# One norm-row buffer spaced over eight score steps, and a second store buffer and a fourth raw buffer for the weights

## The chip, the cores and the metric

The kernel runs on one core of one Trainium2 chip. The metric is the device time of one execution in microseconds; lower is better. Before the change three runs took 1256.49, 1258.76 and 1260.37 us, median 1258.76 us.

## The reference

The program is an attention block, followed by two chained dense blocks, all in float32:

```
attn_setup: batch, n_heads, seq, head_dim = (4, 12, 448, 64)
q_n, k_n = rmsnorm(q, g_q), rmsnorm(k, g_k)        # x / sqrt(mean(x*x) + 1e-6) * g
attn = softmax(1/sqrt(64) * q_n @ k_n^T)
x = (attn @ v), heads joined to (1792, 768)
h = ((x @ w1) * (x @ w2)) @ w3 ; x = h @ w_out      # first block, d_ff 1024
h = x @ w_in ; g = h * clip(h + 3, 0, 6) / 6        # second block, d_ff 2048
out = g @ w_out2
```

The kernel replaces `w3 @ w_out` by one product W' (768 x 1024), which it computes itself while attention runs.

## The kernel before

Attention works on 24 head pairs. A pair takes eight score steps of 112 query rows each, so there are 192 steps; pair i owns steps 8i to 8i+7. A step is: two score matmuls (lines 549 and 550), one VectorE pass that scales the scores by the norms' rows `rb` and takes the row maximum (556), a ScalarE exponential (568), and eight steps later the transposes (575), their split into a high and a low part (584, 594) and the product with V (627, 628).

TensorE gets two kinds of work: these steps, and "filler", cut into groups of three matmuls (lines 81 to 83, the `mm3` helper, which splits a float32 product into three passes). Filler is first W' (`wprime`, 128 groups), then for each batch `layer1` (96 groups, reads `xhl`) and `layer2` (48 groups, reads `abh`). `fill` hands filler out after each step, by a rate in microseconds. Filler needs weights that are converted on the chip: a raw piece (`raw`) comes in by DMA, ScalarE (137, 138) and VectorE (140, 143) turn it into float32, ScalarE takes the high part (203 for W', 287 for layer 1) and GpSimd the low part (205, 289); then the raw buffer is free and the next piece is fetched. Layer 1's converted weights go back to DRAM (`w12d`) and are read again for later batches. W' leaves PSUM in `evac`: ScalarE (223) and VectorE (224) write the store buffer `wst`, and three DMAs store it to `wpd`.

The norms: `load_nat(i)` brings the 112x1024 rows of q and k of pair i, `ssq` squares them in place on ScalarE (446), `ssum` sums them on VectorE (453). For every second pair `rms1`, `rms2`, `small1` and `small2` turn the sums of two pairs into the factors, store them to `rkd`, and `load_rb` reads them back as the rows `rb` that line 556 needs.

Which task is traced at which step stands in the list at the end of `attention` (`at(t, ...)`), moved by the table `SHIFT` (`ssum` one step earlier, `rms1` one later, among others). A scheduler then sets the final order on each engine from its own model of the time: what it holds to be ready first goes first. Filler may not come before the matmuls of three steps earlier (`issue_after`), but it may come much later than where it was traced. Each engine works through its list in order, and SyncE (SP) issues all DMAs, also in order, so an instruction that waits holds all that stand behind it.

After attention the second block runs: conversion and split of its weights with 512 + 512 groups of matmuls, from about 656 us on.

Of the kernel before, what the change touches and what calls it, by code (L numbers as in the profile page):

```python
# [26 lines left out]
P = 128  # L27
CP = 112
# [19 lines left out]
def fused_kernel(ctx: ExitStack, tc: tile.TileContext, nat, qT, kT, vin, gq, gk,  # L48
# [48 lines left out]
    def at(t, fn, *a):  # L97
        tasks[max(t + SHIFT.get(getattr(fn, "__name__", ""), 0), now[0])].append((fn, a))
# [117 lines left out]
    def wprime():  # L216
        pool, place = W["pool"], W["place"]

        def evac(a, n, ps):
            h = NH // P  # L220
            st = pool.tile([P, h, 2, P], F32R, tag="wst", bufs=1, name="wst")
            src = ps[:, :NH].rearrange("p (n c) -> p n c", c=P)
            nc.scalar.activation(st[:, :, 0, :], src, AF.Copy)
            nc.vector.tensor_sub(st[:, :, 1, :], src, st[:, :, 0, :])
            for i in range(h):
                j, c = divmod((n * h + i) * M1 + a, 6)
                dma(wpd[j, :, c], st[:, i].bitcast(F32).rearrange("p t c -> p (t c)"))

        def mul(a, n, c, ps):
            h, l = W["w3"][a, c // 4]  # L230
            cs = slice(c % 4 * P, c % 4 * P + P)
            wh, wl = W["woh"][c, n]
            mm3(ps[:, :NH], h[:, cs], l[:, cs], wh, wl, c == 0, c == M1 - 1)

        def ready(a, n, c):
            return prep[0].ready(place["a", a, c // 4]) and prep[0].ready(place["c", c, n])

        for group in [(0, 1)] + [(a,) for a in range(2, M1)]:
            for n in range(2):
                acc = [bank("f") for _ in group]  # L240
                for c in range(M1):
                    for a, ps in zip(group, acc):
                        while not ready(a, n, c):
                            yield None
                        mul(a, n, c, ps)
                        yield 3 * 0.163
                    if n == 1 and c % 4 == 3:
                        W["free"] += len(group)
                for a, ps in zip(group, acc):
                    later(evac, a, n, ps)  # L250
        yield None
        yield None
        W["cm"].__exit__(None, None, None)
        open_l1()
# [5 lines left out]
    def open_l1():  # L260
        L["cm"] = tc.tile_pool(name="l1", bufs=1, side="right", **RW)
        pool = L["cm"].__enter__()
        raw, ws = defaultdict(list), {}
        L.update(ws=ws, xhl={}, abh={}, cur=0, pool=pool)
        pieces = [(u, h) for u in range(2, 2 * M1) for h in range(2)]
        pieces.reverse()

        def load():
            if pieces:
                u, h = pieces.pop()  # L270
                raw[u].append(fetch(pool, w12[u // 2, 1 - u % 2][:, h * NH : h * NH + NH], NH, "raw", 3))

        def item(u):

            if u < 2:
                ws[u] = W["first"][1 - u]
                return
            r = u % NU
            t = (W["hp"] if u % 5 < 2 else pool).tile([P, 2, DM], F32R, tag="ws", bufs=2 if u % 5 < 2 else 3, name="ws")
            if u < 2 * M1:  # L280
                for h, f in enumerate(raw.pop(u)):
                    cs = slice(h * NH, h * NH + NH)
                    if f.dtype != F32:
                        w = f[:, :, 0]
                        yield from convert(w, f)
                        f = w.bitcast(F32)
                    nc.scalar.activation(t[:, 0, cs], f, AF.Copy)  # L287
                    yield 0.35
                    nc.gpsimd.tensor_sub(t[:, 1, cs], f, t[:, 0, cs])  # L289
                    load()  # L290
                    yield 0.0
                dma(w12d[r // 2, 1 - r % 2], t.bitcast(F32).rearrange("p t c -> p (t c)"))
            else:
                src = w12d[r // 2, 1 - r % 2] if r < 2 * M1 else wpd[r - 2 * M1].rearrange("p k c -> p (k c)")
                dma(t.bitcast(F32).rearrange("p t c -> p (t c)"), src)
                yield 0.0
            ws[u] = t

        for _ in range(3):
            load()  # L300
        prep[0] = Prep([partial(item, u) for u in range(B * NU)], lambda: L["cur"] + AHEAD)
        for _ in range(4):
            prep[0].step()
# [103 lines left out]
    def attention(ap, rate):  # L407
# [2 lines left out]

        def load_nat(i):
            if i < NP:
                T["nat", i] = ap.tile([CP, 4 * NC, D], F32, tag="nat", bufs=2, name="nat")
                a = T.get(("kl", i - 2))
                with ExitStack() as es:
                    if a is not None:
                        es.enter_context(tc.issue_after(a.ins))
                    dma(T["nat", i], nat[i].rearrange("p a b d -> p (a b) d"))
# [241 lines left out]
        groups = {s: [s, s + 1] for s in range(0, NP, 2)}  # L660

        load_nat(0)
        load_nat(1)
        dma(gs[:, 0:1], gq)
        dma(gs[:, 1:2], gk)
        nc.vector.tensor_mul(G, gs[:, 0:1], gs[:, 1:2])
# [25 lines left out]
        for z in range(16):  # L692
            prep[0].step()
        load_nat(2)
        load_nat(3)

        for i in range(NP):
            t = 8 * i
            n = i + 1
            if n < NP:  # L700
                at(t, qhi, n)
                at(t + 1, qlo, n)
                at(t + 2, ksplit, n)
            at(t - 4, load_v, i)
            if i + 2 < NP:
                at(t + 3, load_q, i + 2)
                at(t + 5, load_k, i + 2)
            at(t + 1, vsplit, i)
            if i % 2 == 0 and i + 2 < NP:
                g = groups[i + 2]  # L710
                at(t, ssq, i + 2)
                at(t + 2, ssq, i + 3)
                at(t + 3, ssum, i + 2, g)
                at(t + 3, load_nat, i + 4)
                at(t + 4, ssum, i + 3, g)
                at(t + 4, load_nat, i + 5)
                at(t + 5, rms1, g)
                at(t + 6, rms2, g)
                at(t + 14, load_rb, i + 3)

            u = t + LG
            at(u + 2, rsum1, i)
            at(u + 6, xcopy, i, 0)
            at(u + 7, xadd, i, 0)
            at(u + 8, small1, i, None)
            at(u + 9, small2, i, None)
            at(u + 9, xcopy, i, 1)
            at(u + 10, xadd, i, 1)
            at(u + 14, xout, i)
            if i % 2 == 0 and i + 2 < NP:  # L730
                g = groups[i + 2]
                tasks[t + LG] = [z for z in tasks[t + LG] if z[0] is not small1]
                tasks[t + LG + 1] = [z for z in tasks[t + LG + 1] if z[0] is not small2]
                at(t + LG, small1, i - 1, g)
                at(t + LG + 1, small2, i - 1, g)
# [212 lines left out]
```

## Time and profile before

| | |
|---|---|
| median of three runs | 1258.76 us |
| the profiled execution, its own time | 1259.43 us |
| its span, first to last instruction | 1257.6 us |
| TensorE busy | 1169.0 us (93%) |
| VectorE, ScalarE, GpSimd busy | 753.4, 727.0, 465.0 us |
| mean granted TensorE clock | 0.98 of full speed |
| DMA moved | 203.72 MB |

TensorE is busy nearly all the time in the later two thirds of the span; before about 390 us it is not, and there VectorE and ScalarE are busy for 80 to 90% of the time. So the table's averages hide two parts with different limits, and the rows below are cut by stretches.

### The profile page before, as it was taken

The page shows a single profiled execution, that of the slowest core. Times are in us where ns is not written, and L with a number is a line of the kernel's source. Part 1 is how long each engine was busy: PE and PEld are TensorE (multiplying, and loading weights), DVE is VectorE, ACT ScalarE, POOL GpSimd, SP SyncE. Part 2 cuts the span into 40 slices and gives each one's busy share as a digit, 9 for nine tenths or more (in the row PEclk, how much of TensorE's full clock was granted, in tenths as well). Part 3 has the DMA queues.
Part 4 walks back from the last instruction along what each step waited for, and adds up shares of the span by engine and source line. Part 5 has one row for each costly group of instructions (what it writes and reads, how often), then busy time and mean ns, then how long its engine had stood idle before and what let it go on. Part 6 is the DMA issues. An engine that isn't in the chain of part 4 may idle for free.

```text
span 1257.6 us, 16852 instructions
## 1 busy us (share of the span) xinstructions
PE 1169.0 (93%) x5868; PEld 1024.5 (81%) x5868; DVE 753.4 (60%) x1428; ACT 727.0 (58%) x1401; POOL 465.0 (37%) x292
## 2 busy tenths in 40 slices
PE   3688987887989999999999999899999999999998
PEld 2457976766678999899998998788999999999997
DVE  7887987899884487687623445775433343343332
ACT  6887886888774477677533435664534353444342
POOL 3444343554352022231020003445544554455542
PEclk9798998999999999999999999999999999999999
DMA  8777656598789577666359883440200020001001
GB/s 263 251 224 229 187 176 207 159 280 262 240 274 312 192 242 238 234 218 201 133 197 416 317 302 118 154 156 26 88 1 1 1 88 1 1 1 45 1 1 45
DMA packets 64693, 203.72 MB, mean 162 GB/s; under 512 B 8544, under 2 KB 25440, under 8 KB 64608
## 3 DMA queue, kind: packets, MB, share of 16 engines
q1 hardware_dynamic: 64608, 202.65, 48.4%
q8 instruction: 46, 0.75, 0.2%
q14 instruction: 39, 0.32, 0.1%
HBM read 173.93 MB, written 28.68 MB: 161 GB/s over the span
## 4 chain that ended last, share of the span: by engine, by line
PE 57%; DMA 5%; DVE 3%; ACT 3%; issue 3%; POOL 0%; SPq 0%; ACTq 0%; POOLq 0%; DVEq 0%
PE bank L81 6%; PE bank L82 6%; PE bank L83 6%; PE acc L82 6%; PE acc L81 6%; PE acc L83 6%; PE h L81 5%; PE h L82 5%; PE h L83 5%; DMA wr<-in_win_dram 2%; PE bank L575 2%; DVE wf L143 1%; DMA wr<-in_wo_dram 1%; PE bank L550 1%; PE bank L549 1%
## 5 line engine op out<-in xcount | busy, mean ns | idle before, releaser
L816 POOL TENSOR_TENSOR wis<-wf,wis 128x768 fp32r<-128x768 f32 x63 | 121.2, 1923 | 235.7 <-ACT wis L815 235.7
L888 DVE SCALAR_TENSOR_TENSOR u<-u,h 128x448 f32<-128x448 f32 x64 | 39.6, 618 | 212.1 <-ACT u L887 212.1
L556 DVE CUSTOM_DVE_ANT_0 PP<-bank,rb,rq 112x448 f32<-112x448 f32 x192 | 128.6, 675 | 48.5 <-PE bank L575 28.2
L816 POOL TENSOR_TENSOR wos<-wf,wos 128x768 fp32r<-128x768 f32 x64 | 119.7, 1870 | 98.5 <-ACT wos L815 97.2
L568 ACT ACTIVATE PP<-PP,mx 112x448 f32<-112x448 f32 x192 | 127.6, 666 | 41.3 <-DVE mx L563 33.5
L83 PE MATMUL bank<-xhl,ws 128*128 128x448 f32 x384 | 143.4, 374 | 7.8 <-POOL ws L289 7.7
L81 PE MATMUL bank<-xhl,ws 128*128 128x448 f32 x384 | 143.9, 375 | 4.7 <-ACT ws L287 2.5
L82 PE MATMUL acc<-g,wos 128*128 128x448 f32 x384 | 142.4, 371 | 1.8 <-DVE g L892 1.6
L83 PE MATMUL acc<-g,wos 128*128 128x448 f32 x384 | 141.8, 369 | 0.0
L82 PE MATMUL bank<-xhl,ws 128*128 128x448 f32 x384 | 141.7, 369 | 0.0
L81 PE MATMUL acc<-g,wos 128*128 128x448 f32 x384 | 138.5, 373 | 2.7 <-ACT g L891 2.7
L81 PE MATMUL h<-x2h,wis 128*128 128x448 f32 x378 | 139.3, 368 | 1.1 <-DVE u L888 1.1
L83 PE MATMUL h<-x2h,wis 128*128 128x448 f32 x378 | 138.0, 365 | 2.2 <-POOL wis L816 2.2
L82 PE MATMUL h<-x2h,wis 128*128 128x448 f32 x378 | 139.1, 368 | 0.0
L887 ACT ACTIVATE u<-h,half 128x448 f32<-128x448 f32 x64 | 40.5, 633 | 140.2 <-PE h L83 140.2
L892 DVE TENSOR_TENSOR g<-u,g 128x448 fp32r<-128x448 f32 x64 | 99.5, 1554 | 35.4 <-ACT g L891 35.4
L575 PE MATMUL bank<-ident,PP 112*128 112x112 f32 x672 | 97.2, 267 | 13.0 <-DVE xl L594 8.0
L575 PEld LDWEIGHTS bank<-ident,PP 112*128 112x128 f32 x672 | 79.8, 144 | 34.3 <-issue 10.5
L815 ACT ACTIVATE wos<-wf 128x768 fp32r<-128x768 f32 x64 | 54.0, 844 | 84.9 <-PE acc L83 84.7
L584 ACT ACTIVATE xh<-bank 128x448 fp32r<-128x448 f32 (+1 forms) x156 | 82.4, 539 | 31.8 <-PE bank L575 30.8
L549 PE MATMUL bank<-K,Q 128*112 128x448 f32 x192 | 76.5, 399 | 22.5 <-DVE mx L556 11.2
L594 DVE TENSOR_TENSOR xl<-bank,xh 128x448 fp32r<-128x448 f32 x142 | 86.7, 614 | 14.9 <-ACT xh L584 13.8
(126 smaller groups left out, 2757.5 us busy)
## 6 DMA issues: line engine op xcount, KB each, us to landing
ws<-w12d SPq DMA_DIRECT2D x48, 768.0 KB
ws<-wpd SPq DMA_DIRECT2D x32, 768.0 KB
raw<-in_w_dram SPq DMA_DIRECT2D x32, 384.0 KB
w12d<-ws SPq DMA_DIRECT2D x16, 768.0 KB
wr<-in_win_dram SPq DMA_DIRECT2D x16, 768.0 KB
wr<-in_wo_dram SPq DMA_DIRECT2D x16, 768.0 KB
nat<-in_nat_dram SPq DMA_DIRECT2D x24, 448.0 KB
qr<-in_qT_dram SPq DMA_DIRECT2D x24, 448.0 KB
```

Of the source, the lines that this page charges most:

```text
L81: nc.tensor.matmul(ps, lh, rh, start=first, stop=False)
L82: nc.tensor.matmul(ps, lh, rl, start=False, stop=False)
L83: return nc.tensor.matmul(ps, ll, rh, start=False, stop=last)
L549: nc.tensor.matmul(ps[:CP, :S], qs, k1[:, j, :], start=True, stop=False)
L556: anchors[8 * i + s].append(nc.vector.tensor_tensor_reduce(out=T["PP", i][:, c, sl], in0=ps[:CP, :S], in1=T["rb", i][:, sl], op0=ALU.mult, ...
L568: anchors[8 * i + s].append(nc.scalar.activation(v, v, AF.Exp, bias=T["m", i][:, 8 + s : 9 + s], accum_out=T["sum", i][:, s : s + 1]))
L575: nc.tensor.transpose(ps[:, c * CP : c * CP + CP], src[:, c, kb * P : kb * P + P], ident[:CP, :CP])
L584: nc.scalar.activation(hi, ps, AF.Copy)
L594: nc.vector.tensor_sub(lo, ps, hi)
L815: nc.scalar.activation(t[:, 0, :], wf[q], AF.Copy)
L816: nc.gpsimd.tensor_sub(t[:, 1, :], wf[q], t[:, 0, :])
L892: nc.vector.tensor_sub(g[:, 1, :], u, g[:, 0, :])
```

## The change

`wst` gets two buffers in place of one, and layer 1's `raw` gets four in place of three, with a fourth fetch issued when its pool opens. To make room, `nat` has one buffer in place of two. Since the second pair's rows can't sit beside the first's any more, the first use (pairs 0 and 1) borrows a `PP` buffer for pair 1, the fetch of pair 3 at the start goes away, and in the list of tasks the load of pair i+3 comes at step t and that of pair i+4 at t+4, in place of i+4 at t+3 and i+5 at t+4. The Square of the even pair comes three steps earlier.

```diff
-            st = pool.tile([P, h, 2, P], F32R, tag="wst", bufs=1, name="wst")
+            st = pool.tile([P, h, 2, P], F32R, tag="wst", bufs=2, name="wst")
...
-                raw[u].append(fetch(pool, w12[...][:, h * NH : h * NH + NH], NH, "raw", 3))
+                raw[u].append(fetch(pool, w12[...][:, h * NH : h * NH + NH], NH, "raw", 4))
...
-        for _ in range(3):
+        for _ in range(4):
             load()
...
-                T["nat", i] = ap.tile([CP, 4 * NC, D], F32, tag="nat", bufs=2, name="nat")
+                T["nat", i] = ap.tile([CP, 4 * NC, D], F32, tag="nat", bufs=1, name="nat")
...
         load_nat(0)
-        load_nat(1)
+        x = ap.tile([CP, NC, 2 * S], F32, tag="PP", bufs=2, name="PP")
+        T["nat", 1] = x.rearrange("p a b -> p (a b)")[:, : 4 * NC * D].rearrange("p (a d) -> p a d", d=D)
+        dma(T["nat", 1], nat[1].rearrange("p a b d -> p (a b) d"))
...
         load_nat(2)
-        load_nat(3)
...
-                at(t, ssq, i + 2)
+                at(t - 3, ssq, i + 2)
                 at(t + 2, ssq, i + 3)
-                at(t + 3, ssum, i + 2, g)
-                at(t + 3, load_nat, i + 4)
+                at(t, ssum, i + 2, g)
+                at(t, load_nat, i + 3)
                 at(t + 4, ssum, i + 3, g)
-                at(t + 4, load_nat, i + 5)
+                at(t + 4, load_nat, i + 4)
```

The scheduler makes new lists out of this. Below, the number behind a name tells one buffer's use from another. On TensorE, from the score of step 75 to that of step 77, the list before begins (L81 to L83 on `xhl`, `ws` are layer 1's filler; L549 and L550 the scores, L575 transposes, L627 and L628 the products with V):

```order
L550 MATMUL bank_2644<-K_2454,Q_2233 112x448
L549 MATMUL bank_2691<-K_2453,Q_2233 112x448
L550 MATMUL bank_2691<-K_2454,Q_2233 112x448
L83 MATMUL bank_2621<-xhl_2355,ws_2395 128x448
L81 MATMUL bank_2621<-xhl_2358,ws_2395 128x448
L82 MATMUL bank_2621<-xhl_2358,ws_2395 128x448
L83 MATMUL bank_2621<-xhl_2358,ws_2395 128x448
L81 MATMUL bank_2621<-xhl_2415,ws_2395 128x448
L82 MATMUL bank_2621<-xhl_2415,ws_2395 128x448
L83 MATMUL bank_2621<-xhl_2415,ws_2395 128x448
L628 MATMUL bank_2376<-xl_2371,vo_1950 128x448
```

After the change TensorE's list has, from the second score matmul of step 76 to the first of step 77:

```order
L550 MATMUL bank_2691<-K_2454,Q_2234 112x448
L81 MATMUL bank_2679<-xhl_2418,ws_2542 128x448
L82 MATMUL bank_2679<-xhl_2418,ws_2542 128x448
L83 MATMUL bank_2679<-xhl_2418,ws_2542 128x448
L81 MATMUL bank_2679<-xhl_2471,ws_2542 128x448
L82 MATMUL bank_2679<-xhl_2471,ws_2542 128x448
L83 MATMUL bank_2679<-xhl_2471,ws_2542 128x448
L81 MATMUL bank_2679<-xhl_2474,ws_2542 128x448
L82 MATMUL bank_2679<-xhl_2474,ws_2542 128x448
L83 MATMUL bank_2679<-xhl_2474,ws_2542 128x448
L549 MATMUL bank_2748<-K_2453,Q_2234 112x448
```

At the same score the filler after the change is at `bank_2679`, the product after `bank_2621`: layer 1 moved forward among the steps. Counted over the whole list, the groups of layers 1 and 2 that stand before the second score matmul of the 72nd, 80th, 88th, 96th, 104th, 112th, 120th and 128th step are 12, 21, 40, 57, 70, 84, 110 and 181 before, and 8, 42, 58, 72, 90, 136, 158 and 181 after. From there on the counts agree within two groups; before layer 1, W' has 28 in place of 20 groups ahead of the 24th step and the same number ahead of the 40th, 48th, 56th and 64th.

On ScalarE, at the first evacuation of W' (L223; L203 is a high part of W' weights, L137 and L138 are conversions, L568 an exponential, L446 a Square of `nat`), the list before is:

```order
L203 ACTIVATE woh_469<-raw_352 128x384
L223 ACTIVATE wst_482<-bank_203 128x3x128
L137 ACTIVATE raw_467<-raw_467 128x384
L138 ACTIVATE raw_467<-raw_467 128x384
L584 ACTIVATE xh_551<-bank_546 128x448
L203 ACTIVATE woh_530<-raw_400 128x384
L584 ACTIVATE xh_604<-bank_599 128x448
L568 ACTIVATE PP_592,sum_594<-PP_592,mx_593 112x448 x2
L446 ACTIVATE nat_293<-nat_293 112x1024
L203 ACTIVATE woh_561<-raw_436 128x384
```

After the change ScalarE's list has there:

```order
L223 ACTIVATE wst_480<-bank_201 128x3x128
L203 ACTIVATE woh_467<-raw_350 128x384
L137 ACTIVATE raw_398<-raw_398 128x384
L223 ACTIVATE wst_486<-bank_202 128x3x128
L138 ACTIVATE raw_398<-raw_398 128x384
L584 ACTIVATE xh_426<-bank_421 128x448
```

The second evacuation now comes three rows after the first; before, it came fourteen rows after it, with two exponentials between them.

On SP, where the norms' rows `rb` for pairs 2 and 3 are fetched (`rkd` is their store, `wpd` the store of W'), the list before is:

```order
L89 DMA raw_288<-in_wo_dram 128x768
L89 DMA rkd_58<-rks_415 16x112
L89 DMA raw_313<-in_wo_dram 128x768
L89 DMA rb_480<-rkd_58 112x896
L89 DMA rb_570<-rkd_58 112x896
L89 DMA qr_711<-in_qT_dram 128x896
```

After the change SP's list has there:

```order
L89 DMA nat_628<-in_nat_dram 112x1024
L89 DMA raw_398<-in_wo_dram 128x768
L89 DMA raw_434<-in_wo_dram 128x768
L89 DMA rkd_58<-rks_413 16x112
L89 DMA raw_465<-in_wo_dram 128x768
L89 DMA wpd_62<-wst_480 128x256
L89 DMA rb_478<-rkd_58 112x896
```

The fetch of `rb` now stands behind a fetch of `nat` and behind the first store of W'.

## Rows read from the trace of the kernel before

**Rows 1.** Windows by stage: us, then busy us and (instructions) of PE, PEld, DVE, ACT, POOL

```profile
0.00:70.20 70.20, 37.11 (x139) 23.30 (x139) 53.65 (x115) 52.73 (x109) 28.64 (x25) 0.90 0.75 243
70.20:221.80 151.60, 134.56 (x716) 113.38 (x716) 127.46 (x299) 119.00 (x262) 62.44 (x42) 0.93 0.67 210
...
246.90:372.80 125.90, 105.12 (x528) 82.12 (x529) 113.02 (x262) 104.81 (x236) 56.53 (x43) 0.97 0.79 255
372.80:446.90 74.10, 72.31 (x388) 65.31 (x387) 38.47 (x91) 38.82 (x83) 13.85 (x10) 1.00 0.77 254
446.90:656.00 209.10, 208.83 (x1156) 188.75 (x1155) 146.92 (x366) 134.23 (x290) 44.67 (x32) 1.00 0.63 205
```

**Rows 2.** The same stretches, exponentials of line 568 alone (two instructions each)

```profile
246.90:372.80 125.90, 29.13 (x80) 0.97 0.79 255
372.80:446.90 74.10, 11.63 (x33) 1.00 0.77 254
446.90:656.00 209.10, 48.64 (x128) 1.00 0.63 205
```

**Rows 3.** The same stretches, line 81 alone (one matmul of each filler group)

```profile
246.90:372.80 125.90, 30.45 (x79) 15.29 (x79) 0.97 0.79 255
372.80:446.90 74.10, 31.98 (x88) 16.55 (x88) 1.00 0.77 254
446.90:656.00 209.10, 79.91 (x217) 40.62 (x216) 1.00 0.63 205
```

**Rows 4.** Windows: a stretch of dense DMA, and one of filler alone

```profile
30.00:40.00 10.00, 6.29 (x27) 4.04 (x26) 10.00 (x29) 9.66 (x21) 3.56 (x3) 1.00 1.01 331
...
880.00:900.00 20.00, 20.00 (x100) 18.25 (x99) 9.48 (x12) 10.73 (x17) 9.45 (x5) 1.00 0.00 1
```

**Rows 5.** Tile `wst`: what its instructions waited for, and who waited for them

```profile
  DMA wpd<-wst: 9.8, 4
...
  PE bank L81: 2.2, 2
```

**Rows 6.** Timeline of ScalarE and TensorE at two of these waits

```profile
120.46 0.49 ACT L223 ACTIVATE wst<-bank 128x384 fp32r<-128x384 f32 x1 [3.67 <-DMA wpd<-wst]
...
116.60 0.69 PE L81 MATMUL bank<-woh,w 128*128 128x384 f32 x1 [2.01 <-DVE wst L224]
...
166.59 0.49 ACT L223 ACTIVATE wst<-bank 128x384 fp32r<-128x384 f32 x1 [3.43 <-DMA wpd<-wst]
...
167.57 0.47 PE L627 MATMUL bank<-xh,vo 128*128 128x448 f32 x1 [2.69 <-ACT xh L584]
```

**Rows 7.** Groups of 246.9 to 372.8 us: busy, mean ns, idle before

```profile
L287 ACT ACTIVATE ws<-raw 128x384 fp32r<-128x384 f32 x25 | 13.6, 545 | 0.6 <-DVE raw L143 0.6
L137 ACT ACTIVATE raw<-raw 128x384 f32<-128x384 f32 x23 | 12.8, 558 | 6.9 <-DMA raw<-in_w_dram 6.8
L138 ACT ACTIVATE raw<-raw 128x384 int32<-128x384 uint16 x23 | 12.6, 550 | 0.0
...
L143 DVE SCALAR_TENSOR_TENSOR raw<-raw 128x384 int32<-128x384 int32 x24 | 22.1, 921 | 0.1
...
L140 DVE SCALAR_TENSOR_TENSOR raw<-raw 128x384 int32<-128x384 int32 x24 | 15.8, 657 | 3.5 <-ACT raw L138 1.4 <-issue 1.4 <-POOL ws L289 0.7
...
L83 PE MATMUL bank<-xhl,ws 128*128 128x448 f32 x72 | 28.3, 395 | 6.9 <-POOL ws L289 6.8
```

**Rows 8.** Tile `nat`, waits of its instructions over the whole span

```profile
  DMA nat<-in_nat_dram: 2.9, 2
```

**Rows 9.** Timeline of the start: first `nat` fetches and first Square

```profile
0.74 0.87 SPq L89 DMA_DIRECT2D nat<-in_nat_dram  x2
...
4.57 1.06 ACT L673 ACTIVATE nat<-nat 112x1024 f32<-112x1024 f32 x1 [2.54 <-DMA nat<-in_nat_dram]
```

**Rows 10.** Timeline of VectorE at step 16: first use of pair 2's `rb`

```profile
67.23 0.68 DVE L556 CUSTOM_DVE_ANT_0 PP<-bank,rb,rq 112x448 f32<-112x448 f32 x1
...
69.32 0.54 DVE L224 TENSOR_TENSOR wst<-bank,wst 128x384 fp32r<-128x384 f32 x1
```

More of the change, by code (lines that the diff above doesn't have):

```diff
@@ L270, in load @@
                 u, h = pieces.pop()
-                raw[u].append(fetch(pool, w12[u // 2, 1 - u % 2][:, h * NH : h * NH + NH], NH, "raw", 3))
+                raw[u].append(fetch(pool, w12[u // 2, 1 - u % 2][:, h * NH : h * NH + NH], NH, "raw", 4))
         def item(u):
```

## The prediction

> **What bounds the kernel now.** I read first the windows by stage [rows 1]. From 446.9 us on TensorE is busy without a gap (208.83 of 209.10 us in the first stretch), so whatever is late before that point shifts the end by as much, and what is saved there is saved at the end. Before it, TensorE is idle for 33 us in the start, 17 us in the product W' (70.2 to 221.8 us) and 21 us in the stretch from 246.9 to 372.8 us. There VectorE is busy 113.02 of 125.90 us (90%) and ScalarE 104.81 (83%). The next stretch, 372.8 to 446.9 us, is the reverse: TensorE 98%, VectorE and ScalarE about half.
>
> Then I counted score steps [rows 2] and filler groups [rows 3] in the same stretches: 40 steps and 79 groups in the first, 16 steps (33 instructions, two each) and 88 groups in the second. So the kernel runs steps and conversions first, with TensorE waiting, and then makes up the filler with the others waiting. A group's price is read where filler runs alone: 100 matmuls in 20.00 us [rows 4], 0.20 each, 0.60 for three. A step's price for TensorE is an estimate from the full stretch: 209.1 us less 217 x 0.60, over 64 steps, 1.23 us. By these prices the first stretch holds 79 x 0.60 + 40 x 1.23 = 96.6 us of TensorE work in 125.9 us, the second 88 x 0.60 + 16 x 1.23 = 72.5 in 74.1.
>
> Third come the waits of `wst`: ScalarE stood 9.8 us, four times, for the store of the evacuation before [rows 5]; two of these are 3.67 and 3.43 us long, and beside them TensorE stood 2.01 and 2.69 us [rows 6].
>
> **The change part by part.** All sums go against the profiled execution's own 1259.43 us, which lies 0.7 us above the median of the runs.
>
> *Second `wst` buffer.* An evacuation now waits for the store before the last one, not the last. At most the 9.8 us of ScalarE go. Not all will: TensorE's own idle time at the two large waits is 2.0 and 2.7 us, other waits (for conversions, for transposes) stand behind them, and where three evacuations come close together in the new list, at step 32, the third still waits for the first's store. I take -5, about TensorE's 4.7 us, bounds -10 and 0.
>
> *Order of layer 1's filler, and the fourth raw buffer.* With one more raw piece in flight the scheduler holds the weights to be ready earlier, and puts 128 groups in place of 72 between the 72nd and the 112th step, and 45 in place of 97 between the 112th and 128th. Both lists hold the same 181 at the 128th, so the sum to look at is that of both stretches, 125.9 + 74.1 = 200.0 us. The second becomes 45 x 0.60 + 16 x 1.23 = 46.7 us if TensorE bounds it. The first holds 128 x 0.60 + 40 x 1.23 = 126.0 us of TensorE work; but ScalarE's work grows too, from 104.8 us by 4 conversions of 0.545 + 0.558 + 0.550 us [rows 7] and by the evacuations that come with 56 more groups (five of layer 2, three instructions for layer 1 and five splits of x, 13 of some 0.54 us, an estimate from those in rows 7), to 118 us. At its 83% use that is 142 us. VectorE gets 4 x (0.921 + 0.657) more [rows 7] and some 3 us of evacuation, 122 us; at 90% that is 136. So I take 142 + 47 = 189, a gain of 11. Bounds: TensorE alone, 126 + 47 = 173, a gain of 27; and none, or a loss of 3 us, when the weights are later than the list holds them, for TensorE already stood 6.9 us for GpSimd's low parts in the order of before and ScalarE 6.8 us for raw pieces [rows 7]. The fourth buffer acts through these 6.8 us; they are in the 83%.
>
> *One `nat` buffer.* A pair's rows can be fetched only after the sum of the pair before, two steps ahead of its Square. A fetch takes 3.8 us from issue to the Square's start [rows 9]; a step in the stretch is 125.9 / 40 = 3.1 us, so two steps cover it unless SP is held or the DMA is dense (331 GB/s at a full queue [rows 4]). Behind the Square on ScalarE stand the exponentials, and behind these VectorE's next pass and the transposes. With two buffers, no Square waited for its rows after the start (two waits, 2.9 us, both there [rows 8, 9]). The Trainium skill (DMA: Bandwidth & Descriptors, Rules for kernel authors) says to issue a transfer early and wait for it late, with the computing in between; the change does the opposite, and the trace agrees so far that early issue leaves no wait. By that rule the slow rival below would be the forecast. I take +1, bounds 0 and +15.
>
> *The chain to `rb` of pair 2.* Pair 3's rows now come after pair 2's sum, so the factors are later, and the fetch of `rb` stands behind the first store of W' on SP. In the trace VectorE's evacuation for that store starts at 69.32 us, after the first use of that `rb` at 67.23 us [rows 10]. Were it as late, `rb` would land at about 69.3 + 0.5 + 3.8 = 73.6 us, a loss of 6.4; but the two evacuations now stand ahead of the conversions, and W' is 8 groups further by the 24th step. I take +2, bounds -2 and +7.
>
> *The borrowed `PP` buffer* at the start costs nothing: the same two fetches are issued back to back [rows 9], and the buffer is next used by pair 1, after that sum.
>
> Sum: -5 - 11 + 1 + 2 = -13, 1259.4 - 13 = 1246.4, and 0.7 less against the median: 1246.
>
> The Trainium skill (Perfetto Trace Analysis, Identifying Performance Opportunities) says that the same gap repeating on the engine that should be saturated can mean too few buffers for the next tile, and that regimes with different limits gain from being interleaved. The four waits of `wst` and the two stretches are such cases in this trace; by it alone the sum would be -9.8 and -27, 1223, which leaves out what ScalarE and VectorE still have to do.
>
> **The rivals.** *No gain in layer 1.* Filler moved forward stands ahead of scores on an engine that works in order; if its weights come late, scores wait behind them and VectorE and ScalarE starve. For it: the 6.9 us of waits for low parts with the looser order, and the dense stretch between the 72nd and 80th step, 34 groups, where the pieces have to come about every 3 us, at the end of what the DMA gave [rows 4]. Against it: one more buffer. Then only -5 + 3 is left: 1257, no change that can be told.
>
> *Slower: the Square waits for its rows.* Six odd pairs (5 to 15) have their Squares before the 128th step. If the two steps don't cover the fetch because SP stands at another wait in front of it, ScalarE stands for most of the 3.8 us, say 3 each, 18 us, and the rows of `rb` behind it come late as well; with half the gains left (-8) that is +10, 1268. It decides from about 2 us per Square, where it eats the 13 us. For it: with one buffer each fetch stands on SP behind VectorE's sum. Against it: two steps of cover.
>
> *More than forecast.* Layer 1's stretch becomes bound by TensorE, -25 with `wst`'s 5: about 1233.
>
> **How the numbers follow.** Forecast 0.52 (its own range 1238 to 1255), no gain 0.18, slower 0.18, more 0.12. About 0.3%, 3.8 us, is what a measurement of this kernel can tell from no change. Faster: nearly all of the forecast and of the last case, 0.61; same 0.20; slower 0.19. The range for 8 in 10 runs from the last case to a little beyond no change, 1233 to 1264; beyond it lie most of the slow rival and the best of the fast one.
>
> **What would show it.** In the changed profile: `wst`'s waits for `wpd` well under 9.8 us; the 129th exponential's start at about 434 us in place of 446.9, with the distance from there to the end the same within 2 us; in the stretch from the 73rd to the 113th exponential some 128 filler groups in about 142 us, TensorE over 85% busy; no Square of `nat` waiting over 1.5 us on a DMA; the first use of pair 2's `rb` before 72 us. The forecast is wrong if `nat` stands among ScalarE's waits with over 8 us, if TensorE's waits for low parts rise beyond 15 us, or if the time after the 128th step has changed.

## The result, and the profile after

The changed kernel takes 1245.53 us (median of four runs, 1242.23 to 1247.39) against 1258.58 us of the kernel before beside it: ratio 0.9888, 95% interval 0.9863 to 0.9913, or 13.1 us faster. The profiled execution took 1246.62 us, its span is 1244.8.

First the windows by stage, cut at the same steps as in [rows 1] (the start of the 17th, 65th, 73rd, 113th and 129th exponential; the last window ends at 656 us in both). Columns are as there.

```profile
0.00:80.50 80.50, 43.48 (x157) 28.57 (x158) 60.31 (x122) 55.65 (x114) 31.11 (x27) 0.85 0.75 241
80.50:224.80 144.30, 130.61 (x702) 109.36 (x701) 124.00 (x296) 115.91 (x257) 55.67 (x39) 0.94 0.64 201
...
250.10:387.80 137.70, 128.74 (x661) 107.51 (x661) 112.78 (x262) 109.38 (x243) 57.05 (x44) 0.98 0.85 281
387.80:437.40 49.60, 48.91 (x269) 43.21 (x268) 40.06 (x95) 33.33 (x71) 12.75 (x8) 1.00 0.73 236
437.40:656.00 218.60, 217.98 (x1200) 197.17 (x1199) 143.21 (x365) 136.24 (x295) 45.77 (x34) 1.00 0.66 216
```

Four differences matter. The start is 10.3 us longer (80.5 for 70.2). W', 17th to 65th, is 7.3 shorter (144.3 for 151.6), so that the 73rd exponential comes 3.2 later. From the 73rd to the 129th exponential it is 137.7 + 49.6 = 187.3 us in place of 125.9 + 74.1 = 200.0, 12.7 less. Behind that it is 1244.8 - 437.4 = 807.4 in place of 810.7, 3.3 less. In the stretch from the 73rd on TensorE's work is the same (128.74 + 48.91 = 177.65 us; before 105.12 + 72.31 = 177.43), so what went is its idle time, from 22.6 to 9.65 us.

The filler did move forward: line 81 alone in the same two stretches, as in [rows 3], has 119 groups and then 48, where it had 79 and 88.

```profile
250.10:387.80 137.70, 44.60 (x119) 22.81 (x118) 0.98 0.85 281
387.80:437.40 49.60, 17.78 (x48) 9.15 (x49) 1.00 0.73 236
```

The groups of the 40 steps, which answer to [rows 7]: TensorE's third matmul no longer waits for GpSimd's low part (6.8 us before), while ScalarE's waits for raw pieces went only from 6.8 to 5.8.

```profile
L83 PE MATMUL bank<-xhl,ws 128*128 128x448 f32 x74 | 28.6, 386 | 0.0
...
L287 ACT ACTIVATE ws<-raw 128x384 fp32r<-128x384 f32 x23 | 12.6, 549 | 2.2 <-DVE raw L143 2.0
L137 ACT ACTIVATE raw<-raw 128x384 f32<-128x384 f32 x22 | 12.1, 550 | 5.8 <-DMA raw<-in_w_dram 5.8
```

What waits for `wst`'s store [rows 5], and what waits for `nat` behind the start [rows 8]: one wait of 5.4 us in place of four of 9.8 together, and one Square of 2.2 us, of which there was none before.

```profile
  DMA wpd<-wst: 5.4, 1
```

```profile
  ACT nat L446: 2.2, 1
```

The timeline of SP and of VectorE at step 16 (start, duration, engine, line), which answers to [rows 10]: the first use of pair 2's `rb` is at 76.43 us in place of 67.23.

```profile
65.67 0.33 SPq L89 DMA_DIRECT2D rkd<-rks  x1
67.26 0.33 SPq L89 DMA_DIRECT2D wpd<-wst  x1
68.67 0.33 SPq L89 DMA_DIRECT2D rb<-rkd  x1
69.05 2.51 SPq L89 DMA_DIRECT2D wpd<-wst  x5
72.09 0.45 SPq L89 DMA_DIRECT2D rb<-rkd  x1
...
76.43 0.68 DVE L556 CUSTOM_DVE_ANT_0 PP<-bank,rb,rq 112x448 f32<-112x448 f32 x1 [2.71 <-PE bank L575]
```

The pace of layer 1's weights is best read at their 28 high parts (line 287). The first three before, and four after, come from pieces fetched as the pool opens. From the fourth at 250.47 us, or the fifth at 248.36, to the last they follow a cycle: fetch, conversion, high part, low part, next fetch into the freed buffer. The last one of each kernel, before and after:

```profile
367.80 0.56 ACT L287 ACTIVATE ws<-raw 128x384 fp32r<-128x384 f32 x1 [0.30 <-DVE raw L143]
```

```profile
346.72 0.55 ACT L287 ACTIVATE ws<-raw 128x384 fp32r<-128x384 f32 x1
```

That is (367.80 - 250.47) / 24 = 4.89 us a piece with three buffers, (346.72 - 248.36) / 23 = 4.28 with four; times the buffers, one buffer turned round in 14.7 and 17.1 us. Three buffers at the longer turnaround would be slower still, so the count sets the pace, though not alone. The quotient is a turnaround only while the order keeps the buffers in use: in run 2 below, which asks for the weights late, four buffers give (368.18 - 247.84) / 23 = 5.23 us a piece, or 20.9.

### The profile page after: what moved, and what is told of

Same layout as the page of the kernel before. It is cut to its first block, busy times and chain, and to the rows that moved or that the text cites. A ratio compares the mean times of both kernels' runs of the same rounds, so it can differ in the third digit from the quotient of the medians.

```text
span 1244.8 us, 16876 instructions
## 1 busy us (share of the span) xinstructions
PE 1166.1 (94%) x5868; PEld 1024.6 (82%) x5868; DVE 753.5 (61%) x1428; ACT 726.7 (58%) x1401; POOL 459.1 (37%) x292
## 4 chain that ended last, share of the span: by engine, by line
PE 64%; DVE 12%; DMA 9%; ACT 8%; issue 6%; POOL 0%; SPq 0%; ACTq 0%; DVEq 0%; POOLq 0%
PE bank L81 7%; PE bank L83 7%; PE bank L82 7%; PE acc L81 6%; PE acc L82 5%; PE acc L83 5%; PE h L81 5%; PE h L82 5%; PE h L83 5%; PE bank L575 3%; DVE PP L556 2%; ACT PP L568 2%; DMA wr<-in_win_dram 2%; DVE Q L523 2%; PE bank L549 2%
## 5 line engine op out<-in xcount | busy, mean ns | idle before, releaser
L568 ACT ACTIVATE PP<-PP,mx 112x448 f32<-112x448 f32 x192 | 127.6, 666 | 51.9 <-DVE mx L563 42.4
L81 PE MATMUL bank<-xhl,ws 128*128 128x448 f32 x384 | 143.6, 374 | 3.4 <-ACT bs L316 1.7
L83 PE MATMUL bank<-xhl,ws 128*128 128x448 f32 x384 | 142.7, 372 | 0.0
L81 PE MATMUL acc<-g,wos 128*128 128x448 f32 x384 | 137.2, 369 | 5.6 <-ACT g L892 5.5
L83 PE MATMUL acc<-g,wos 128*128 128x448 f32 x384 | 141.2, 368 | 0.0
L83 PE MATMUL h<-x2h,wis 128*128 128x448 f32 x378 | 137.7, 364 | 2.3 <-POOL wis L817 2.3
L81 PE MATMUL h<-x2h,wis 128*128 128x448 f32 x378 | 139.1, 368 | 0.6 <-DVE u L889 0.6
L575 PE MATMUL bank<-ident,PP 112*128 112x112 f32 x672 | 97.1, 268 | 16.5 <-DVE xl L594 12.7
L575 PEld LDWEIGHTS bank<-ident,PP 112*128 112x128 f32 x672 | 80.6, 145 | 37.5 <-DVE xl L594 13.3
L549 PE MATMUL bank<-K,Q 128*112 128x448 f32 x192 | 76.7, 401 | 25.8 <-DVE Q L523 12.7
```

The lines of the kernel that those rows point to most:

```text
L81: nc.tensor.matmul(ps, lh, rh, start=first, stop=False)
L83: return nc.tensor.matmul(ps, ll, rh, start=False, stop=last)
L549: nc.tensor.matmul(ps[:CP, :S], qs, k1[:, j, :], start=True, stop=False)
L568: anchors[8 * i + s].append(nc.scalar.activation(v, v, AF.Exp, bias=T["m", i][:, 8 + s : 9 + s], accum_out=T["sum", i][:, s : s + 1]))
L575: nc.tensor.transpose(ps[:, c * CP : c * CP + CP], src[:, c, kb * P : kb * P + P], ident[:CP, :CP])
```

## The experiments

Theory A: the order of the filler makes the gain. Theory B: the fourth raw buffer does, whatever the order. Theory C: each only with the other. All times are medians; steps are starts of the (n+1)th exponential in the profiled execution; "idle" is TensorE's in steps 72 to 128, "clock" its mean granted clock there, "raw wait" ScalarE's for raw pieces there. The kernel before had medians of 1260.02, 1260.53, 1258.84 and 1259.29 us beside runs 1 to 4, 5 to 8, 9 to 11 and 12. The profiled execution is one of the runs and lies up to 5.0 us from the median (run 1: 1263.39; run 12: 1225.97), so a stretch of one kernel is read with that margin.

| kernel | `wst`, `raw` | time | ratio to before | step 16 | 72 | 128 | 72 to 128 | idle | clock | raw wait |
|---|---|---|---|---|---|---|---|---|---|---|
| before | 1, 3 | 1258.58 | | 70.2 | 246.9 | 446.9 | 200.0 | 22.6 | 0.98 | 6.8 |
| changed | 2, 4 | 1245.53 | 0.9888 | 80.5 | 250.1 | 437.4 | 187.3 | 9.7 | 0.98 | 5.8 |
| 1 before, order forced | 1, 3 | 1258.37 | 0.9992 | 70.7 | 248.2 | 453.0 | 204.8 | 19.6 | 0.93 | 20.2 |
| 2 changed, late filler | 2, 4 | 1269.98 | 1.0081 | 79.5 | 249.6 | 457.2 | 207.6 | 25.8 | 0.91 | 1.2 |
| 3 `nat` part alone | 1, 3 | 1262.44 | 1.0020 | 76.4 | 258.8 | 454.7 | 195.9 | 15.8 | 0.96 | 17.6 |
| 4 changed, pair 3 early | 2, 4 | 1237.78 | 0.9826 | 77.4 | 242.5 | 429.5 | 187.0 | 8.5 | 0.97 | 6.4 |
| 5 changed, order forced | 2, 4 | 1242.44 | 0.9849 | 80.2 | 251.6 | 435.0 | 183.4 | 9.5 | 0.96 | 2.1 |
| 6 as 5, three raw | 2, 3 | 1257.87 | 0.9964 | 80.1 | 253.9 | 452.0 | 198.1 | 17.8 | 0.95 | 12.7 |
| 7 changed, one `wst` | 1, 4 | 1245.81 | 0.9871 | 77.0 | 255.5 | 435.2 | 179.7 | 7.0 | 0.99 | 6.8 |
| 8 changed, three raw | 2, 3 | 1261.54 | 1.0017 | 78.3 | 247.6 | 451.2 | 203.6 | 16.9 | 0.92 | 9.2 |
| 9 as 5, one `wst` | 1, 4 | 1243.84 | 0.9882 | 75.1 | 254.4 | 432.5 | 178.1 | 8.1 | 1.00 | 3.5 |
| 10 as 4, order forced | 2, 4 | 1237.38 | 0.9823 | 76.8 | 245.6 | 427.4 | 181.8 | 10.0 | 0.97 | 2.6 |
| 11 as 4, five raw | 2, 5 | 1242.62 | 0.9867 | 79.1 | 251.3 | 426.9 | 175.6 | 5.0 | 1.00 | 0.0 |
| 12 as 11, room shared | 2, 5 | 1230.24 | 0.9777 | 76.4 | 244.8 | 419.1 | 174.3 | 4.0 | 1.00 | 0.0 |

**1. The order alone, on the kernel before.** The last filler matmul of each step is kept in a table, and the scores of steps 72 to 127 are held behind it.

```diff
-            ps = score(*divmod(t, 8)) if live else None
+            with ExitStack() as es:
+                if live and 72 <= t < 128 and marks.get(t - 2):
+                    es.enter_context(tc.issue_after(marks[t - 2].ins))
+                ps = score(*divmod(t, 8)) if live else None
```

> The kernel before with its buffers (two for nat, one for wst, three raw), but the scores of steps 72 to 127 have to stand behind the filler handed out two steps earlier, so that TensorE's list has 45, 69, 90, 116 and 138 groups of layers 1 and 2 ahead of steps 80 to 112, in place of 24, 42, 57, 73 and 85. Theory A (the order of filler among the steps is what shortened the stretch from step 72 to 128): the stretch falls from 200 us to about 187, the end to about 1246 us. Theory B (the fourth raw buffer did it, the list only follows): with three raw buffers the weights come late, TensorE's waits for low parts rise from 7 to 15 us or more, the stretch stays at about 200 us and the time within 4 us of 1258.6.

Measured: 1258.37, interval of the ratio 0.9972 to 1.0013. The order alone gains nothing. The group of the first conversion (its line is 141 here; steps 72 to 128) shows why: with filler forward the kernel is at the weights' heels, and ScalarE waits three times as long for them.

```profile
L141 ACT ACTIVATE raw<-raw 128x384 f32<-128x384 f32 x23 | 12.7, 554 | 20.2 <-DMA raw<-in_w_dram 20.2
```

**2. The changed kernel, filler late.** The rate function returns less filler for steps 70 to 111 and more for 112 to 131.

```diff
+        if 70 <= t < 112:
+            return 1.0, 2
+        if 112 <= t < 132 and len(marks) < 184:
+            return 3.6, 4
```

> The changed kernel with all its buffers, but the filler is handed out more slowly over steps 70 to 111 and faster after, so that TensorE's list has 27, 41, 55, 70, 88, 129 and 174 groups ahead of steps 80 to 128, near the list before (24, 42, 57, 73, 85, 112, 184) and not the changed one (42, 60, 73, 90, 138, 161, 184). Theory A (order): the stretch from step 72 to 128 goes back to about 198 us, the end to about 1256 us. Theory B (fourth raw buffer): it stays at about 187 us and the time at 1246 us.

Measured: 1269.98, 1.0052 to 1.0109. Four buffers with late filler lose; ScalarE hardly waits for raw pieces (1.2 us), and TensorE is idle for 25.8 us. Its list is near that of the kernel before (88 groups ahead of step 112 and 129 ahead of step 120, where that has 85 and 112 by the same count). So the buffer gains nothing without an order that uses it (against B). This late list was not run with three buffers: how much of the loss is the list's own stays open.

**3. The `nat` part alone**, on the kernel before.

```diff
-                T["nat", i] = ap.tile([CP, 4 * NC, D], F32, tag="nat", bufs=2, name="nat")
+                T["nat", i] = ap.tile([CP, 4 * NC, D], F32, tag="nat", bufs=1, name="nat")
...
-                at(t + 3, load_nat, i + 4)
+                at(t, load_nat, i + 3)
```

> The change with its nat part alone: one buffer, respaced loads, pair 1 in a PP buffer; wst has one buffer and raw three, as before. TensorE's list is nevertheless the forward one from step 72 on (42, 57, 66, 101 and 138 groups ahead of steps 80 to 112). Theory A (order): the start is late by some 10 us as in the changed kernel, W' keeps its waits for the store (about 5 us more than the changed kernel), the stretch from step 72 is as short as in the changed kernel: about 1251 us. Theory B (buffers): nothing is gained and the start is lost: about 1268 us.

Measured: 1262.44, 1.0001 to 1.0039: 2.4 us slower, step 16 at 76.4. This part, without a fourth raw buffer, already makes the scheduler's list go forward (138 groups ahead of step 112; before 85 by the same count), and ScalarE waits 17.6 us for raw pieces in it. So the forward order needs no fourth buffer; the prediction had put it down to that buffer. It is no property of this part either: with `wst`'s second buffer added (run 8) the list goes back to 90 groups ahead of step 112. At step 72 this run is 11.9 us later than the kernel before (258.8 for 246.9); from there on it regains most of that.

**4. Pair 3's rows at the start.** They go into a buffer of V (`vo`) that is not needed yet, and the later fetch is left out.

```diff
+        T["nat", 3] = ap.tile([P, 2, 4, 2, D], F32, tag="vo", bufs=2, name="vo")[:CP]...
+        dma(T["nat", 3], nat[3].rearrange("p a b d -> p (a b) d"))
...
-                at(t, load_nat, i + 3)
+                if i:
+                    at(t, load_nat, i + 3)
```

> The changed kernel, with pair 3's rows fetched at the start into a buffer of the V tiles, which pair 1's V needs only later. If the late step 16 (80.5 us against 70.2) comes from pair 3's rows having to wait for pair 2's sum, step 16 comes at about 71 us. If that is carried to the end: about 1238 us. Rival: the steps up to 32 wait for W' weights anyway, the gain shrinks as the loss did (10 us at step 16, 3 us at step 64): about 1243 us. Second rival: step 16 waits for the store of W' in front of rb on SP's list, and stays at about 78 us: 1245 us.

Measured: 1237.78, 0.9794 to 0.9859; 7.75 us less than the changed kernel. Both fetches of `rb` stand ahead of the stores of W' again, as the timeline shows:

```profile
63.14 0.80 SPq L89 DMA_DIRECT2D rb<-rkd  x2
68.68 2.89 SPq L89 DMA_DIRECT2D wpd<-wst  x6
72.35 0.68 DVE L556 CUSTOM_DVE_ANT_0 PP<-bank,rb,rq 112x448 f32<-112x448 f32 x1
```

Of the 7.75 us step 16 shows 3.1 and steps 16 to 72 another 4.5 (165.1 for 169.6). The total is the expected one, the way to it is not: step 16 was to come at 71 us and came at 77.4, since its exponential stands behind conversions, high parts and transposes' splits on ScalarE's list, 5 us after the pass on VectorE. What shortens steps 16 to 72 was not separated. The Trainium skill's rule to issue a transfer early and wait late (DMA: Bandwidth & Descriptors, Rules for kernel authors) holds for this one fetch, which stood in a chain; for the 22 Squares behind the start the late issue cost 2.2 us in all.

**5 and 6. One order, four raw buffers and three.** The diff of run 1 on the changed kernel; run 6 has in addition:

```diff
-                raw[u].append(fetch(..., "raw", 4))
+                raw[u].append(fetch(..., "raw", 3))
```

> The changed kernel (four raw buffers) with the scores of steps 72 to 127 held behind the filler that was traced two steps earlier: 45, 69, 90, 116, 138, 161 and 184 groups stand before the 80th, 88th, 96th, 104th, 112th, 120th and 128th step. Theory C (order and fourth raw buffer pay only together): steps 72 to 128 stay near the changed kernel's 187 us (184 to 191), 1243 to 1249 us in all; ScalarE waits under 8 us there for raw pieces. Theory A (the order alone pays, and only its exact form failed in the run on the old buffers): the same, about 1246, so this run tells A from C only beside the next one. Were the scheduler's own list the better one for the waits, it would be 195 us and 1254.

> The same order of scores and filler (45, 69, 90, 119, 138, 161, 184 groups) with the change's other parts, but three raw buffers in place of four: the buffer alone at one list. Theory C: ScalarE waits 15 to 20 us for raw pieces between the 72nd and the 128th step, the stretch takes 197 to 205 us, the whole 1256 to 1262. Theory A (order): waits of 6 us, 187 us, 1246, like the run with four.

Measured: 1242.44 (0.9803 to 0.9896) and 1257.87 (0.9936 to 0.9992). At nearly one list of TensorE (the counts are those of the expectations) the buffer is worth 15.4 us. Theory A falls, and with run 2 against B, theory C is left. ScalarE's waits with three buffers are 12.7 us, less than the 15 to 20 expected. The windows of steps 72 to 128, with four and then with three:

```profile
251.60:435.00 183.40, 173.88 (x917) 151.41 (x915) 152.61 (x351) 142.30 (x311) 74.37 (x50) 0.96 0.82 270
```

```profile
253.90:452.00 198.10, 180.30 (x916) 153.44 (x915) 152.58 (x352) 142.42 (x312) 70.02 (x51) 0.95 0.79 255
```

VectorE and ScalarE do the same work in both; TensorE is idle for 9.5 and 17.8 us. The high parts follow each other in 3.71 and 4.38 us, a turnaround of 14.8 and 13.1.

**7 and 9. What the second `wst` buffer is worth**, in the scheduler's order (7) and the forced one (9).

```diff
-            st = pool.tile([P, h, 2, P], F32R, tag="wst", bufs=2, name="wst")
+            st = pool.tile([P, h, 2, P], F32R, tag="wst", bufs=1, name="wst")
```

> The changed kernel with one wst buffer: what the second store buffer is worth. My sum put it at -5 (0 to -10); so 1250.5 is expected, with 10 to 15 us of ScalarE's waits for the store, and steps 16 to 72 (169.6 us in the changed kernel) 5 us longer, 175. If the second buffer is hidden behind other waits: 1245 to 1247 and 170 us.

> The run with four raw buffers and the scores of steps 72 to 127 held behind the filler (1242.4 us), with one wst buffer in place of two: the second store buffer at nearly one list (48, 73, 90, 118, 141, 162, 187 groups before steps 80 to 128). Without the forced order that buffer was worth nothing (1245.8 against 1245.5). If its 5 us of my sum are there but a poorer order of layer 1, which the scheduler makes with it, takes them back: 1246 to 1248 here, the exponential of step 72 some 4 us later, and 72 to 128 about 183 us. If the waits for the store are hidden behind others: 1242 and 183 us, with step 72 no later or the time regained behind it.

Measured: 1245.81 (0.9818 to 0.9924) and 1243.84 (0.9853 to 0.9911), against 1245.53 and 1242.44 with two: worth 0.3 and 1.4 us, neither to be told from nothing. Both lie under the 5 of the sum; with four to six runs each, a gain of a few microseconds isn't excluded. The waits come back as expected (10.0 us, four times, in run 7), and in run 7 steps 16 to 64 take 148.3 us in place of 144.3. But step 16 is 3.5 us earlier with one buffer (77.0 for 80.5; 75.1 for 80.2 in the forced order). The timeline of run 7 shows the start of that:

```profile
66.83 0.33 SPq L89 DMA_DIRECT2D rb<-rkd  x1
67.21 0.93 SPq L89 DMA_DIRECT2D wpd<-wst  x2
68.66 0.47 SPq L89 DMA_DIRECT2D rb<-rkd  x1
73.00 0.68 DVE L556 CUSTOM_DVE_ANT_0 PP<-bank,rb,rq 112x448 f32<-112x448 f32 x1 [1.01 <-DMA rb<-rkd]
```

With one `wst` two stores stand between the two fetches of `rb`, with two buffers five do. So a part of what the buffer saves in W' goes at step 16. That the stores alone do it was not tried: in the changed kernel the last to be waited for at 76.43 us was TensorE's transposes.

The rest goes after step 72. There the kernels with two buffers are still ahead, by 5.4 us (changed and run 7), 2.8 (5 and 9) and, with three raw buffers, 11.2 (8 and 3); but from 72 to 128 they take 7.6, 5.3 and 7.7 us longer. The changed kernel and run 7 over that stretch, and the last high part in run 7, which with two buffers came at 346.72:

```profile
250.10:437.40 187.30, 177.65 (x928) 150.72 (x928) 152.84 (x356) 142.71 (x313) 69.80 (x51) 0.98 0.82 269
```

```profile
255.50:435.20 179.70, 172.66 (x921) 148.81 (x919) 142.91 (x351) 138.07 (x307) 65.56 (x50) 0.99 0.84 283
...
334.05 0.54 ACT L287 ACTIVATE ws<-raw 128x384 fp32r<-128x384 f32 x1
```

The weights came no earlier for the earlier step 72, in none of the three pairs (332.54 for 329.22; 367.10 for 364.90). Of the longer stretch only 2.6, 1.4 and 1.1 us are TensorE's idle time; the rest is its busy time, with 7, 3 and 9 more recorded matmuls and at a lower mean clock each time (0.98, 0.96, 0.92 for 0.99, 1.00, 0.96). The scheduler's lists differ too (7 and 3 are further forward). Which of these costs the gain was not tried.

**8. The changed kernel with three raw buffers**, in the scheduler's own order for it (the diff of run 6 alone).

> The changed kernel with three raw buffers, in the scheduler's own order for it (33, 46, 57, 75, 90, 161, 184 groups before steps 80 to 128, in place of 42, 58, 72, 90, 136, 158, 184): what the fourth raw buffer is worth. Theory C: -8 to -12 of the change's -13 go, 1253 to 1258, ScalarE's waits for raw pieces over 12 us between steps 72 and 128. If wst makes most of the gain: 1247 to 1250.

Measured: 1261.54, 0.9992 to 1.0041. All of the change's gain goes, 16.0 us; more than expected, with shorter raw waits (9.2) than expected. Its list is the looser one, so buffer and order change together here; only runs 5 and 6 hold the order. TensorE's idle time, 16.9 us, is only 7 more than in the changed kernel; the other 9 us are its work itself, 186.66 us in place of 177.65 for the same 928 matmuls, at a clock of 0.92:

```profile
247.60:451.20 203.60, 186.66 (x928) 158.45 (x927) 152.14 (x353) 142.78 (x315) 68.42 (x52) 0.92 0.77 251
```

**10. Both**: pair 3 early and the forced order (the diffs of 4 and 1 together).

> The version with pair 3's rows fetched at the start (1237.8 us), with the scores of steps 72 to 127 held behind the filler as well (45, 69, 90, 116, 138, 161, 184 groups in place of 42, 60, 73, 90, 138, 161, 184). From the same step without that fetch (1245.5 to 1242.4) 3 us are expected: 1235, steps 72 to 128 in 184 us in place of 187. If the two lists are alike in worth: 1238 and 187.

Measured: 1237.38, 0.9793 to 0.9852. The stretch is 5 us shorter, step 72 is 3 later, and the total is that of run 4. With four buffers the forced order is worth nothing that can be told.

**11 and 12. Five raw buffers.** Theory D: buffers over turnaround set the pace of the weights. In run 11 the room comes from one `bs` and one `rks` buffer:

```diff
-                raw[u].append(fetch(..., "raw", 4))
+                raw[u].append(fetch(..., "raw", 5))
...
-            bs = pool.tile([P, S], F32, tag="bs", bufs=2, name="bs")
+            bs = pool.tile([P, S], F32, tag="bs", bufs=1, name="bs")
...
-                sb = ap.tile([16, CP], F32, tag="rks", bufs=2, name="rks")
+                sb = ap.tile([16, CP], F32, tag="rks", bufs=1, name="rks")
```

> The version with pair 3's rows fetched at the start (1237.8 us), with five raw buffers; room comes from one buffer in place of two for bs (layer 1's first product) and for rks. Theory D: a piece's buffer turns round in 15 to 17 us (5.8 to 7 fetch, 7 to 8 conversion and low part, 1.5 to the next issue), and the weights come at that time over the number of buffers, 4.9 us each with three, 4.1 with four; with five it would be 3.3, the last high part at some 325 us in place of 338, and 72 to 128 in 175 to 182 us, 1227 to 1234 in all. If the DMA, at 87% of its time with four, is the next limit, the fetch lengthens to 9 us and more, and it stays at 184 to 188 us, 1235 to 1239. One bs buffer may cost: waits of over 5 us for bs would show that.

Measured: 1242.62, 0.9837 to 0.9897: slower than run 4. The stretch took 175.6 us, as D had it (175 to 182), at 3.59 us a piece (3.3 expected); but step 72 came 8.8 us later, and the time behind step 128 was 815.1 for 807.0. Who waited for `bs`, over the whole span:

```profile
  PEld bank L81: 13.1, 9
```

Run 12 keeps two `rks`, and puts `bs` tiles into the raw buffers from the second batch and from layer 2 on, where those are free (the calls of `small_tile` and what it shares with run 11 are left out here):

```diff
+    def small_tile(pool, b):
+        if b == 0:
+            return pool.tile([P, S], F32, tag="bs", bufs=1, name="bs")
+        t = pool.tile([P, NH, 2], I32, tag="raw", bufs=5, name="raw")
+        return t.rearrange("p n t -> p (n t)")[:, :S].bitcast(F32)
...
-            t = ap.tile([CP, w], F32, tag="rt", bufs=2, name="rt")
+            t = ap.tile([CP, w], F32, tag="rt", bufs=1, name="rt")
```

> Five raw buffers on the version with pair 3's rows fetched at the start (1237.8 us), without the two costs that the run with one bs and one rks buffer had: rks keeps two, bs has one buffer only for layer 1 of the first batch, and all its later tiles go into the raw buffers, which are free by then (the room for the fifth comes from that and from one buffer for rt, which only VectorE writes and reads). In the run before, steps 72 to 128 took 175.6 us in place of 187.0, but step 72 came 8.8 us later and the time after step 128 was 8.1 longer, with 13.1 us of TensorE's waits for bs. Theory D and these two causes: step 72 at 243 us, 72 to 128 in 175 to 178, behind it 807, so 1226 to 1229 in all. If the later step 72 or the longer end come from the fifth buffer itself (its transfers at 93% of the DMA's time): one of the two stays, 1233 to 1238.

Measured: 1230.24 (1225.97 to 1233.52), 0.9739 to 0.9814, the fastest of all; 29 us under the kernel before beside it and 15 under the changed one. The window of steps 72 to 128, the group of the first conversion there, and the last high part:

```profile
244.80:419.10 174.30, 170.35 (x916) 147.09 (x915) 143.51 (x343) 136.01 (x302) 68.63 (x49) 1.00 0.86 286
```

```profile
L137 ACT ACTIVATE raw<-raw 128x384 f32<-128x384 f32 x19 | 10.5, 551 | 0.0
```

```profile
317.52 0.56 ACT L287 ACTIVATE ws<-raw 128x384 fp32r<-128x384 f32 x1
```

No conversion waits for a raw piece, the last high part is 29 us earlier than in the changed kernel, and TensorE is idle for 3.95 us of 174.3 at the full clock. It is now the bound here too; the DMA, 86% busy over the stretch, has 14% of its time left. Step 72 (244.8 us, 243 expected) and the time behind step 128 (804.9, 807 expected) show that neither cost of run 11 came from the fifth buffer itself.

## Why the prediction was right or wrong

The time (1246 forecast) and the sum (-13 against -13.1) came out, by luck in so far as two of its terms were wrong and cancelled. By stretches of the profiled executions it is the same: at step 72 the forecast was -2 (-5 + 1 + 2) and +3.2 came, from 72 to 128 it was -11 and -12.7 came, and behind that 0 and -3.3.

*Second `wst` buffer, -5.* Failed. The row on which it rests, 9.8 us of waits, is right as a row; steps 16 to 64 gained 4.0 us by it, and step 72 came 2.8 to 11.2 us earlier. The step that failed is "what is saved there is saved at the end": layer 1's stretch, 72 to 128, took 5.3 to 7.7 us more and the gain was gone before step 128. Missed was also that an earlier evacuation brings its stores earlier onto SP. Runs 7 and 9: 0.3 and 1.4 us, none that can be told. Why the stretch behind takes the gain back stays open.

*Order of layer 1 and fourth raw buffer, -11.* The stretch gained 12.7 us, in the two parts that were forecast (137.7 + 49.6 against 142 + 47), TensorE 93% busy in the first (over 85% asked), 119 groups there (128 forecast). But the mechanism was mis-sized. The step that failed is inside: "The fourth buffer acts through these 6.8 us; they are in the 83%". It acts through the cycle of fetch, conversion and release, of which those waits are the small part that this order shows. Take the buffer away and 15.4 us (runs 5, 6) or 16.0 us (8) go; leave the order and take it as in 1, and nothing is gained. The term is -16, not -11, and it belongs to the buffer as long as the order offers it work (2). The forward order does not come from the buffer alone: the `nat` part has it too (3). Against the kernel before, the stretch shows only 12.7 of the 16: run 8 took 203.6 us for it, the kernel before 200.0, which is within what single executions differ by.

*One `nat` buffer, +1, and the chain to `rb`, +2.* Together +3 against +2.4 in run 3, whose interval just excludes no change. The Squares' share is right: one waited, 2.2 us, over the 1.5 named as a sign. The chain was undersized where it can be seen: 9.2 us later at its first use, where +7 was the bound for the term, with 6.2 us at step 16 and 11.9 at step 72 for the `nat` part alone (3). The stretches from step 72 on gave most of it back.

So the change by its parts, added one after the other: +2.4 (3), then -0.9 for `wst` (8 less 3), then -16.0 for `raw` with the order that it brings (changed less 8), -14.5 in all; with the -13.1 measured side by side this agrees within what the medians of the kernel before differ by among these runs, 2 us.

*The time behind step 128* was to stay within 2 us and shrank by 3.3; runs 1 to 10, whose program there is all but the same, have 806.4 to 809.2 us, so nothing is read from it.

*The rivals.* "No gain in layer 1" named the right danger, late weights; run 1 is that case, and the fourth buffer was what kept it away. The slow rival, Squares that wait, did not come: two steps covered the fetch. "More than forecast", 1233 by a TensorE-bound layer 1, needed the fifth buffer and pair 3's rows at the start (12). Of the rule cited from the Trainium skill (Perfetto Trace Analysis, Identifying Performance Opportunities), that a gap repeating on the engine that should be saturated can mean too few buffers, the runs agree for `raw` and not for `wst`: its gap shrank from 9.8 to 5.4 us and the time did not follow. Both gaps stood on ScalarE, 78% (119.00 of 151.60 us) and 83% busy in their stretches.

## What to carry to other kernels

Read a chain of buffers by its turnaround: the time between two points of the trace, divided by the items handled in it, times the number of buffers (here 4.89 us x 3 = 14.7). Where the consumer would take items faster than that, another buffer pays more than the waits in the trace show, since the order has been slack enough to hide most of them. That holds only while all buffers are in use and the order offers the work. And a time saved in one stretch counts only when the next stretches don't take it back: compare two kernels at every border between stretches, here steps 16, 72 and 128, before a saving is added to a sum. A buffer that lets a store go earlier should also be followed onto the queue that it shares with other transfers.

## What the hardware showed beside this

A wait can cost twice, once as idle time and once through the clock. Windows of 10 us of run 8, columns as above, the clock third from the right:

```profile
250.00:260.00 10.00, 10.00 (x54) 8.66 (x53) 8.55 (x21) 7.93 (x20) 3.11 (x3) 1.00 1.01 354
260.00:270.00 10.00, 7.42 (x39) 5.69 (x37) 8.74 (x17) 9.84 (x22) 5.47 (x5) 0.98 0.63 199
270.00:280.00 10.00, 9.59 (x42) 8.23 (x42) 9.14 (x28) 7.83 (x18) 2.75 (x2) 0.68 0.86 295
```

TensorE was busy for 7.42 of 10 us, and in the next 10 us the clock granted to it was 0.68 of full, a mean of its two levels, 1.2 and 2.4 GHz; its busy time there is 9.59 us for 42 matmuls, where 10.00 us hold 54 at the full clock. The timeline of TensorE shows the same in single matmuls (start, duration):

```profile
266.50 0.36 PE L82 MATMUL bank<-xhl,ws 128*128 128x448 f32 x1
...
270.41 0.74 PE L628 MATMUL bank<-xl,vo 128*128 128x448 f32 x1 [2.72 <-DVE xl L594]
...
273.22 0.57 PE L82 MATMUL bank<-xhl,ws 128*128 128x448 f32 x1
...
276.67 0.37 PE L82 MATMUL bank<-xhl,ws 128*128 128x448 f32 x1
```

Behind one wait of 2.72 us the same matmul takes 0.57 us, and at 276.67 it takes 0.37 again. So a high busy share can hide a slow engine. Not every gap does it: in the kernel before TensorE was busy for 7.24 us from 270 to 280 us, and the clock stayed at 1.00 there and in the next 10 us. In run 12 the clock stays at 1.00 over the whole stretch, which is part of its gain (170.35 us of TensorE work for 916 recorded matmuls against 177.65 for 928).
